# Moving the last two of a block's eight weight subtractions from GpSimd to VectorE

## The chip, the cores and the metric

The kernel runs on one core of one Trainium2 chip. The metric is device time in microseconds (us), from one execution to the next of the whole program. Five engines work side by side, each through its own queue of instructions, strictly in order: TensorE (PE for matmuls, PEld for weight loads in the profile), VectorE (DVE), ScalarE (ACT), GpSimd (POOL) and SyncE (SP, which here issues most DMAs). Semaphores order the work between them.

## The reference, cut to what matters

An attention layer whose queries are pooled in pairs is followed by a mixture of 8 experts. Each of the 2304 tokens goes to the one expert with the highest gate.

```python
x = softmax(scale * pool(q) @ k.T) @ v            # 4 x 8 heads -> 2304 tokens of 512
expert_idx = argmax(normalised(x) @ normalised(emb).T / tau)
for e in range(8):
    mask = expert_idx == e
    h = np.maximum(x[mask] @ w1[e], 0.0)          # 512 -> 1024
    out[mask] = gate_w[mask, None] * (h @ w2[e])  # 1024 -> 512
```

## The kernel before, in words

The attention stage fills the first 500 us and is not touched. Then the tokens, sorted by expert, are worked in blocks of 128 rows; every block belongs to one expert. With these inputs 21 blocks run, called block 0 to block 20 here. The first five belong to the most frequent expert and share one set of weights.

To keep precision, a float32 weight is held as two 16-bit tensors: a high part in fp16 and a low part in bf16, the difference. The weights of a block come from HBM as eight pieces of 128x1024 float32 (512 KB each): four of w1 and four of w2, in the staging tile `ld` (`st1`, `st2`). For each piece, `cast` (lines 775 to 784) makes the high part on ScalarE (line 782) and then the low part by a TENSOR_TENSOR subtraction (line 784), on GpSimd if the table `PCAST` names the piece and on VectorE otherwise. `PCAST` has six rows: w1 and w2 of the steady blocks (here from block 6 on), of blocks 0 and 1, and of block 5. Weights are converted anew for each block from block 5 on, also where the expert has not changed; the load of a piece (line 761) is skipped by a condition in that case. The last conversion is that of a block 21 which isn't run.

A block takes 96 matmuls of 128 columns, `mm1` (line 804, three products for the high and low parts), a `relu` in two halves, and 24 matmuls of 512 columns, `mm2` (line 827). Each half of the relu is one ScalarE instruction (line 810) and one VectorE instruction (line 811) that makes the low part of the hidden values; the second half's ScalarE instruction waits for the first half's VectorE instruction. `fin` scales the result on ScalarE (line 834) and scatters it by an indirect DMA from GpSimd's queue (line 835); `gather` (line 765) fetches the rows of a later block the same way.

The order is written out by hand in `seg`. In the round of block j it is: mm1 of block j+1; conversion of piece 0 of w1 of block j+2; fin of j-1; gather; piece 1; relu half 0 of j+1; pieces 2 and 3; loads of w1 of j+3; relu half 1 of j+1; mm2 of j; the four pieces of w2 of block j+1; loads of w2 of j+2. So TensorE does mm1 of j+1, mm2 of j, mm1 of j+2, mm2 of j+1, and so on. The converted weights have two sets of buffers (`ws`). After the last round each engine reads the number of blocks from memory (line 908) and branches (line 898): with 21 blocks the branch leads to mm2 and fin of block 20 alone.

Of the kernel before, what the change touches and what calls it, by code (L numbers as in the profile page):

```python
# [42 lines left out]
def attn_moe(ctx: ExitStack, tc: tile.TileContext, qt, kt, vt, emb, tau, w1, w2, out):  # L43
# [262 lines left out]
    RD = 3  # L306
    CUTS = [21, 22, 23, 24]
    WP = 4
    PCAST = [[2], [2], [0, 2, 3], [0, 1, 2, 3], [0, 1, 2, 3], [1]]
    VPOS = [0, 2, 3, 6]  # L310
    QPOS = [1, 2, 3, 3, 5, 7, 8]
    MPOS = [0, 0, 0, 7]
# [430 lines left out]
    def moe():  # L743
# [30 lines left out]
        def cast(j, which, *parts):  # L774
            if j >= NBLK or EB <= j < NS:
                return
            for i in parts:
# [4 lines left out]
                nc.scalar.activation(out=dh, in_=src, func=AF.Copy)  # L782
                eng = nc.gpsimd if i in PCAST[which + (2 if j < EB else 4 if j <= NS else 0)] else nc.vector
                eng.tensor_tensor(out=dl.bitcast(BF16), in0=src, in1=dh, op=ALU.subtract)  # L784
# [341 lines left out]
```

## Time and profile before

| what | value |
|---|---|
| median of 3 runs | 751.28 us (750.44 to 754.35) |
| profiled execution, its own time | 752.46 us |
| its span, first to last instruction | 750.7 us |
| mean granted TensorE clock, share of full speed | 0.955 |

The profile is of one execution. A row of the timeline gives a start (us from the span's start), a duration, the engine, the line of the kernel, the operation, what is written and read, and how many instructions of that kind in a row are merged; brackets give idle time before it and what ended it. Instructions of one engine can overlap by about a tenth of a us, so the cost of one in a row of its kind is read from starts, not from a single duration.

### The profile page before, as it was taken

Reading aid. Unit: us, or ns where it says so; the run is one execution under the profiler, and the core shown is the slowest. Engines: PE = TensorE matmul, PEld = TensorE weight load, DVE = VectorE, ACT = ScalarE, POOL = GpSimd, SP = SyncE. Lnnn points to the kernel's source line nnn. Section 1 sums busy time; section 2 is a strip of 40 time slices with the busy share of each in tenths; the row PEclk is TensorE's granted clock in tenths of the full one; section 3 lists DMA queues with packets and bytes.
Section 4 is the critical chain, followed back from the end, with each engine's and each line's share of the span. In section 5 each row is a group of like instructions: output and inputs, shape, how many; then the busy total and the mean of one; then the engine's idle time right before and its main releaser. Section 6 shows DMA issues by size and latency. Waiting matters only on the chain. (4 is left out here: it accounts for less than half of the span.)

```text
span 750.7 us, 21971 instructions
## 1 busy us (share of the span) xinstructions
PE 658.3 (88%) x8915; PEld 479.6 (64%) x8915; DVE 618.4 (82%) x975; ACT 480.3 (64%) x801; POOL 508.1 (68%) x347
## 2 busy tenths in 40 slices
PE   8798889998889988889989887869998998989883
PEld 3266767776667766677767666837756666665651
DVE  5579998889889888898887997471459999999986
ACT  2455667686676677577667465422647797777874
POOL 5567788887679877678857545652835766668654
PEclk9589999999999999999989998889999999999997
DMA  7724425557532569443375049519899655233581
GB/s 210 202 65 119 135 61 146 163 93 191 163 95 83 159 127 215 134 136 85 120 186 147 15 164 166 97 31 257 274 280 269 180 162 174 55 75 84 158 185 38
DMA packets 80524, 106.97 MB, mean 142 GB/s; under 512 B 50862, under 2 KB 54606, under 8 KB 80416
## 3 DMA queue, kind: packets, MB, share of 16 engines
q1 hardware_dynamic: 76160, 94.47, 48.1%
q0 software_dynamic: 3600, 11.03, 4.8%
q8 instruction: 72, 1.18, 0.7%
q14 instruction: 36, 0.29, 0.1%
q10 hardware_dynamic: 656, 0.00, 0.0%
HBM read 116.44 MB, written 10.23 MB: 169 GB/s over the span
## 5 line engine op out<-in xcount | busy, mean ns | idle before, releaser
L295 POOL TENSOR_TENSOR ar<-ar 128x576 f16<-128x576 f32 x175 | 232.6, 1340 | 112.4 <-ACT ar L293 112.1
L293 ACT ACTIVATE ar<-st 128x576 f32<-128x576 f32 x288 | 186.3, 650 | 120.3 <-PE st L291 112.8
L291 PE MATMUL st<-ar 128*128 128x288 f16 (+1 forms) x1152 | 195.6, 296 | 5.1 <-ACT ar L293 5.1
L784 DVE TENSOR_TENSOR ar<-ld,ar 128x1024 bf16<-128x1024 f32 x100 | 176.2, 1806 | 15.0 <-ACT ar L782 14.9
L370 PE MATMUL acc<-ar 128*128 128x65 f16 (+1 forms) x1440 | 167.3, 194 | 4.7 <-POOL ar L295 2.5
L368 PE MATMUL acc<-ar 128*128 128x65 f16 (+1 forms) x1440 | 167.4, 196 | 0.0
L369 PE MATMUL acc<-ar 128*128 128x64 f16 (+1 forms) x1440 | 167.0, 197 | 0.0
L259 DVE TENSOR_REDUCE mc<-m 128x1 f32<-128x512 f32 (+2 forms) x224 | 140.7, 653 | 26.3 <-PE m L248 17.7
L368 PEld LDWEIGHTS <-ar 128*128 128x128 bf16 (+1 forms) x1440 | 137.8, 99 | 34.8 <-issue 24.0
L782 ACT ACTIVATE ar<-ld 128x1024 f16<-128x1024 f32 x144 | 142.6, 1049 | 14.6 <-DMA ld<-in_w_dram 13.4
L369 PEld LDWEIGHTS <-ar 128*128 128x128 bf16 (+1 forms) x1440 | 137.7, 99 | 20.1 <-issue 2.1
L784 POOL TENSOR_TENSOR ar<-ld,ar 128x1024 bf16<-128x1024 f32 x44 | 99.5, 2268 | 66.6 <-ACT ar L782 53.5
L370 PEld LDWEIGHTS <-ar 128*128 128x128 f16 (+1 forms) x1440 | 138.0, 101 | 6.3 <-DVE ar L295 3.3
L804 PE MATMUL hps<-ar 128*128 128x128 f16 x2016 | 122.7, 220 | 17.6 <-POOL ar L784 9.5
L804 PEld LDWEIGHTS <-ar 128*128 128x128 f16 (+1 forms) x2016 | 115.3, 98 | 27.4 <-DVE ar L784 11.1
L291 PEld LDWEIGHTS <-ar 128*128 128x128 f16 (+1 forms) x1152 | 99.9, 100 | 37.4 <-issue 15.1
L827 PE MATMUL ops<-ar 128*128 128x512 f16 (+1 forms) x504 | 116.3, 388 | 7.4 <-DVE ar L784 3.9
L295 DVE TENSOR_TENSOR ar<-ar 128x576 f16<-128x576 f32 x113 | 113.6, 1006 | 0.5 <-ACT ar L293 0.5
L827 PEld LDWEIGHTS <-ar 128*128 128x128 f16 x504 | 49.3, 100 | 65.4 <-issue 9.6
L248 PE MATMUL m<-ar 128*128 128x512 f16 (+1 forms) x280 | 71.9, 319 | 10.3 <-DVE mc L259 8.8
L257 DVE CUSTOM_DVE_ANT_0 my<-m,my 128x512 bf16<-128x512 f32 x56 | 38.5, 688 | 24.8 <-PE m L248 13.8
L810 ACT ACTIVATE ar<-hps 128x512 f16<-128x512 f32 x38 | 22.6, 595 | 51.1 <-DVE ar L811 36.3
(180 smaller groups left out, 705.6 us busy)
## 6 DMA issues: line engine op xcount, KB each, us to landing
ld<-in_w_dram SPq DMA_DIRECT2D x156, 512.0 KB
ld<-in_q_dram SPq DMA_DIRECT2D x16, 576.0 KB
ld<-in_v_dram SPq DMA_DIRECT2D x16, 576.0 KB
ar<-ld SPq DMA_DIRECT2D x31, 288.0 KB
ld<-in_k_dram SPq DMA_DIRECT2D x15, 576.0 KB
ar<-ld SPq DMA_DIRECT2D x33, 144.0 KB
ar<-qhl SPq DMA_DIRECT2D x32, 144.0 KB
xs<-xh SPq DMA_DIRECT2D x13, 256.0 KB
```

Source lines behind the costliest of these rows:

```text
L248: nc.tensor.matmul(out=o, lhsT=qr[:, c:c + 128], rhs=kr[r], start=True, stop=True)
L259: nc.vector.tensor_reduce(out=mc[p, h][:, j, ts[0]:ts[0] + n], in_=m[:, 0:n * w].rearrange("p (t k) -> p t k", t=n), axis=AX.X, op=ALU.max)
L291: nc.tensor.matmul(out=st[:, a, 0:HQ], lhsT=KK[s][0:n, h, k, c * 128:(c + 1) * 128], rhs=QQ[s][0:n, h, k, a * HQ:(a + 1) * HQ], start=(k = ...
L293: nc.scalar.activation(out=e.rearrange("p (a q) -> p a q", a=2), in_=st[:, :, 0:HQ], func=AF.Exp, scale=1.0 / 16)
L295: return lambda: eng.tensor_tensor(out=EL[g % 2][:, c], in0=e, in1=hi(e), op=ALU.subtract)
L368: nc.tensor.matmul(out=a[r], lhsT=hi(e[:, w]), rhs=VV[s][:, c, h, 0:65], start=(x == 0), stop=False)
L369: nc.tensor.matmul(out=a[r, 0:64], lhsT=hi(e[:, w]), rhs=VV[s][:, c, h, 65:129], start=False, stop=False)
L370: nc.tensor.matmul(out=a[r], lhsT=el[:, w], rhs=VV[s][:, c, h, 0:65], start=False, stop=(x == NC - 1))
L782: nc.scalar.activation(out=dh, in_=src, func=AF.Copy)
L784: eng.tensor_tensor(out=dl.bitcast(BF16), in0=src, in1=dh, op=ALU.subtract)
L804: nc.tensor.matmul(out=hp[j, f][:, t * 128:t * 128 + 128], lhsT=wv(w, i % 2, c)[:, u], rhs=xt[:, 2 * c + i // 2], start=(c == 0 and t == 0 ...
L827: nc.tensor.matmul(out=op[j], lhsT=ht[:, c // 4, i // 2, (c % 4) * 128:(c % 4) * 128 + 128], rhs=wv(w, i % 2, c), start=(k == 0), stop=(k ...
```

## The change

Two entries of the table that says which pieces GpSimd subtracts are emptied: those of w1 and w2 of the steady blocks, which had one piece each (piece 2).

```diff
-    PCAST = [[2], [2], [0, 2, 3], [0, 1, 2, 3], [0, 1, 2, 3], [1]]
+    PCAST = [[], [], [0, 2, 3], [0, 1, 2, 3], [0, 1, 2, 3], [1]]
```

VectorE's program in the steady rounds, before (ar is the tile of the converted weights and hidden values, hps the result of mm1; L784 are subtractions, L811 the relu halves):

```order
L811 SCALAR_TENSOR_TENSOR ar<-hps,ar 128x512
L784 TENSOR_TENSOR ar<-ld,ar 128x1024
L811 SCALAR_TENSOR_TENSOR ar<-hps,ar 128x512
L784 TENSOR_TENSOR ar<-ld,ar 128x1024 x5
L811 SCALAR_TENSOR_TENSOR ar<-hps,ar 128x512
```

and after:

```order
L811 SCALAR_TENSOR_TENSOR ar<-hps,ar 128x512
L784 TENSOR_TENSOR ar<-ld,ar 128x1024 x2
L811 SCALAR_TENSOR_TENSOR ar<-hps,ar 128x512
L784 TENSOR_TENSOR ar<-ld,ar 128x1024 x6
L811 SCALAR_TENSOR_TENSOR ar<-hps,ar 128x512
```

Between the halves of a relu there are now two subtractions (pieces 2 and 3 of w1) where there was one (piece 3), and behind the second half six (four of w2, then pieces 0 and 1 of the next w1) where there were five.

GpSimd's program in the same rounds, before (out_dram is the result, xs the sorted rows in HBM):

```order
L784 TENSOR_TENSOR ar<-ld,ar 128x1024 x2
L835 DMA out_dram<-ar,six 2304x512
L765 DMA ar<-xs,gix 128x513
L784 TENSOR_TENSOR ar<-ld,ar 128x1024 x2
L835 DMA out_dram<-ar,six 2304x512
```

and after:

```order
L835 DMA out_dram<-ar,six 2304x512
L765 DMA ar<-xs,gix 128x513
L835 DMA out_dram<-ar,six 2304x512
L765 DMA ar<-xs,gix 128x513
L835 DMA out_dram<-ar,six 2304x512
```

Only the indirect DMAs of fin and gather stay there. TensorE's and ScalarE's programs are the same in both kernels.

## Rows read from the trace of the kernel before

**Rows 1.** The page: busy time of each engine, share of the span, instructions.

```profile
PE 658.3 (88%) x8915; PEld 479.6 (64%) x8915; DVE 618.4 (82%) x975; ACT 480.3 (64%) x801; POOL 508.1 (68%) x347
```

**Rows 2.** Windows (start:end, length): busy us per engine, granted clock, DMA share, GB/s.

```profile
533.20:554.30 21.10, 21.10 (x245) 15.44 (x243) 14.51 (x10) 12.31 (x15) 13.62 (x7) 1.00 0.91 231
554.30:593.50 39.20, 33.26 (x364) 23.20 (x362) 32.42 (x23) 30.26 (x36) 22.77 (x13) 1.00 0.90 268
593.50:723.70 130.20, 119.71 (x1322) 84.86 (x1320) 127.40 (x89) 98.81 (x117) 84.75 (x43) 1.00 0.46 129
```

**Rows 3.** Groups by line, 592.5 to 711.3: busy, mean ns | idle before.

```profile
L784 DVE TENSOR_TENSOR ar<-ld,ar 128x1024 bf16<-128x1024 f32 x61 | 108.8, 1827 | 2.2 <-ACT ar L782 2.2
...
L784 POOL TENSOR_TENSOR ar<-ld,ar 128x1024 bf16<-128x1024 f32 x20 | 45.0, 2248 | 32.1 <-ACT ar L782 31.8
```

**Rows 4.** Timeline of TensorE, 530 to 573.

```profile
533.21 5.34 PE L827 MATMUL ops<-ar 128*128 128x512 f16 x24
...
543.75 5.34 PE L827 MATMUL ops<-ar 128*128 128x512 f16 x24
...
564.53 0.84 PE L804 MATMUL hps<-ar 128*128 128x128 f16 x12 [2.15 <-POOL ar L784]
...
568.93 4.38 PE L827 MATMUL ops<-ar 128*128 128x512 f16 x19
```

**Rows 5.** Timeline of TensorE, 609 to 636.

```profile
612.56 0.84 PE L804 MATMUL hps<-ar 128*128 128x128 f16 x12 [1.17 <-POOL ar L784]
...
623.40 1.51 PE L804 MATMUL hps<-ar 128*128 128x128 f16 x24 [0.37 <-DVE ar L784]
```

**Rows 6.** Timeline of VectorE, 610 to 655.

```profile
610.02 3.57 DVE L784 TENSOR_TENSOR ar<-ld,ar 128x1024 bf16<-128x1024 f32 x1
...
623.86 1.21 DVE L784 TENSOR_TENSOR ar<-ld,ar 128x1024 bf16<-128x1024 f32 x1
625.00 0.68 DVE L811 SCALAR_TENSOR_TENSOR ar<-hps,ar 128x512 f16<-128x512 f32 x1
625.60 2.35 DVE L784 TENSOR_TENSOR ar<-ld,ar 128x1024 bf16<-128x1024 f32 x2
```

**Rows 7.** Timeline of VectorE in three short stretches, 614 to 631.

```profile
614.12 3.88 DVE L784 TENSOR_TENSOR ar<-ld,ar 128x1024 bf16<-128x1024 f32 x2
...
619.06 4.28 DVE L784 TENSOR_TENSOR ar<-ld,ar 128x1024 bf16<-128x1024 f32 x2
...
628.38 2.64 DVE L784 TENSOR_TENSOR ar<-ld,ar 128x1024 bf16<-128x1024 f32 x1 [0.44 <-ACT ar L782]
```

**Rows 8.** Timeline of GpSimd, 610 to 655.

```profile
610.37 2.14 POOL L784 TENSOR_TENSOR ar<-ld,ar 128x1024 bf16<-128x1024 f32 x1
613.64 2.14 POOL L784 TENSOR_TENSOR ar<-ld,ar 128x1024 bf16<-128x1024 f32 x1 [1.14 <-ACT ar L782]
```

**Rows 9.** Timeline of ScalarE, 544 to 562.

```profile
558.60 0.67 ACT L834 ACTIVATE ar<-ops,ar 128x512 f32<-128x512 f32 x1
559.17 1.05 ACT L782 ACTIVATE ar<-ld 128x1024 f16<-128x1024 f32 x1
560.12 0.58 ACT L810 ACTIVATE ar<-hps 128x512 f16<-128x512 f32 x1
560.60 2.00 ACT L782 ACTIVATE ar<-ld 128x1024 f16<-128x1024 f32 x2
```

**Rows 10.** The end: timeline of TensorE and GpSimd, 700 to 751.

```profile
723.61 5.34 PE L827 MATMUL ops<-ar 128*128 128x512 f16 x24
732.36 0.38 PE L827 MATMUL ops<-ar 128*128 128x512 f16 x1 [3.41 <-ACT ar L782]
736.68 7.10 PE L827 MATMUL ops<-ar 128*128 128x512 bf16 x23 [3.95 <-DVE ar L784]
...
744.91 1.01 POOL L835 DMA_INDIRECT out_dram<-ar,six  x1 [1.76 <-POOLq L898]
```

**Rows 11.** Instructions of line 898: queue, count, ns min/median/max, first and last start.

```profile
L898 PEldq COMPARE_BRANCH  x1: 4559/4559/4559, 727.7 to 727.7; - x1
```

## The prediction

> **What bounds the kernel now.** I read the page's busy times first, then windows over the expert stage, then the groups by line there, and last the timelines of single engines over two blocks.
>
> The page [rows 1] shows TensorE busy for 88% of the span and VectorE for 82%. That is a mean over stages, so windows come next [rows 2]. There are three different stretches. From 533.2 to 554.3 TensorE is busy all the time: 21.10 of 21.10 us. From 593.5 to 723.7 VectorE is busy for 127.40 of 130.20 us, 98%, and TensorE for 92%. Between them, from 554.3 to 593.5, the DMA engines are at 0.90 and move 268 GB/s, the weights of several experts one after another. The clock is 1.00 in all three.
>
> In the long last stretch VectorE is the bound. TensorE waits there inside mm1 for low parts that are not yet subtracted, 1.17 us for GpSimd's piece in one block and 0.37 us for VectorE's in the next [rows 5]. The second relu half on ScalarE waits for VectorE too.
>
> Is VectorE full of its own work? No. A subtraction alone takes 1.21 us; two in a row take 2.35, so each further one costs 1.14; a relu half is followed by the next instruction 0.60 us after its start [rows 6]. Yet the mean over 61 subtractions is 1.827 us [rows 3]. The long ones are those during which GpSimd subtracts. The one at 610.02 takes 3.57 us; GpSimd's runs from 610.37 to 612.51, and VectorE's ends 1.08 us later [rows 6, 8]. The others of the same two blocks show the same: the pair at 614.12 takes 3.88 where 2.35 is normal, the pair at 619.06 takes 4.28, the single one at 628.38 takes 2.64 [rows 7]. While GpSimd subtracts, VectorE's subtraction stands still. The lost time is 2.36 + 1.53 + 1.93 + 1.43 = 7.25 us in two blocks, 3.6 us a block. GpSimd's two subtractions take 2 x 2.25 us [rows 3], so most of what it works VectorE pays for.
>
> **The change, part by part.** It removes two subtractions a block from GpSimd and adds two to VectorE. What VectorE has to do in a block was 6 x 1.14 + 2 x 0.60 = 8.0 us of its own and 3.6 us of standing still, 11.6 us, and with its short waits the period of 11.9 us: mm2 of block 6 starts at 568.93 and mm2 of block 19 at 723.61 [rows 4, 10], 154.68 us for 13 blocks, 11.90 each. After the change it is 8 x 1.14 + 2 x 0.60 = 10.3 us, with no stop.
>
> Next is TensorE. Where it isn't held up, mm2 starts follow each other after 543.75 - 533.21 = 10.54 us [rows 4]. That is more than 10.3, so TensorE becomes the bound by a little. ScalarE has eight conversions at 0.95 us, two relu halves at 0.48 and a fin at 0.57, all by starts [rows 9]: 9.1 us. GpSimd keeps only its two indirect DMAs.
>
> Does the order let TensorE run through? Count from the end of mm1 of block j+1. ScalarE's relu half ends at about 0.8, VectorE's at 1.4, pieces 2 and 3 of the next w1 are subtracted by 3.7 (4.1 with the wait of 0.44 for ScalarE that [rows 7] shows). TensorE does mm2 of j meanwhile, 5.2 us, then starts the next mm1, which wants piece 2 after a quarter of its first half and piece 3 later; it would have to wait only if VectorE were over 3 us late. The second relu half and the four pieces of w2 are done at 4.3 and at about 9; the mm2 that needs them starts at 10.5. So nothing is left to wait for in the steady state, and VectorE, with 10.3 against 10.54, makes up a delay of 0.24 us in each block.
>
> The blocks: 13 x (11.90 - 10.54) = 17.7 us. At the entry mm1 of block 7 waits 2.15 us for GpSimd's piece, which itself waits for the load [rows 4]; VectorE would deliver it some 1.1 us earlier. Against that, with earlier work the loads between 560 and 590 come closer to being late; with the DMA at 0.90 I set 1.1 us against the 1.1 us and put the entry at nothing. Its ends are +2 and -4 us: all of the wait gained, or the whole gain of blocks 7 to 9 given back to the DMA (3 x 1.36).
>
> The end: before, mm2 of block 20 starts 8.75 us after mm2 of block 19 (732.36 against 723.61), because TensorE's branch takes 4.56 us from 727.7 on [rows 10, 11]. This stays. Then it stands for 4 us until VectorE has subtracted piece 0 of w2, which had two of GpSimd's pieces in front of it; the other 23 matmuls begin at 736.68 and take 7.10 us, in part at the low clock, 1.2 GHz. Now that piece is ready 5.4 to 5.8 us after the start of mm2 of block 19 (4.3 for the relu, and one subtraction), before the branch is through, and the others at 1.14 us intervals. So the 24 matmuls take 5.34 us from +8.75 and end at +14.1, where they ended at 743.78, +20.2. That is 6.1 us if the clock holds through the 3.4 us of the branch and 4.1 if it falls as before (7.10 against 5.34 x 23/24). The nearest row is the window from 554.3: TensorE is idle for 5.9 us of it in pieces and the clock stays at 1.00 [rows 2]; I take 6.1. ScalarE's four conversions of the unused block end by about +10.6 (the last staging piece is free at +9.2, and one conversion) and don't delay fin; the four extra subtractions there on VectorE hold up nobody. What follows the last matmul is the same.
>
> **The sum.** 17.7 + 6.1 = 23.8 us from the profiled execution's 752.46 is 728.7. The median is 1.18 us below that execution; the same gain from it would give 727.5. I predict 728.5 us.
>
> **A rule that speaks against a part of it.** The row: VectorE's instruction at 610.02 starts 0.35 us before GpSimd's at 610.37 and is still the one that is stretched, by 2.36 us [rows 6, 8]. The Trainium skill, "SBUF — State Buffer", section "Who interferes with whom", has both engines contend for one port pair when VectorE reads two inputs from SBUF, which agrees, but says that the one that issues first holds it and the other blocks. By that rule this one stretch would have another cause and would stay; by the rows it goes like the other three. It is the third rival below.
>
> **Rivals.**
> First, hand-offs between the engines keep the period above TensorE's own. For it: every block has the chain ScalarE, VectorE, ScalarE, VectorE in the relu, and today TensorE still waits 0.37 us where only VectorE delivers. Against it: those waits come from a VectorE that is late all the time. If about 0.6 us remain in each block, the period is 11.1, the gain 13 x 0.8 = 10.4, with 4.1 at the end 14.5 us: 738.0.
> Second, the loads bind in blocks 7 to 9: 4 us less, 724 to 733, or 732.7 from the sum. It lies inside the range.
> Third, the stretch of the instruction that started first isn't GpSimd's doing. Then 2.36 us in two blocks stay, VectorE needs 10.3 + 1.2 = 11.5 us a block, and 13 x 0.4 + 4.1 = 9.3 us are gained: 743.
> Fourth, and slower: the long subtractions come from VectorE's own traffic (the staging tile being filled while it is read, say) and not from GpSimd, so VectorE takes two more of the mean kind. Two at even 1.14 us added to a full engine are 2.28 us a block, 13 x 2.28 = 29.6 us: 782. It decides once eight subtractions average more than (11.9 - 1.2) / 8 = 1.34 us. Against it: each of the four long ones in two blocks lies on one of GpSimd's, and those that lie on none take 1.21.
> That the change doesn't move what it says is excluded by the order of the two programs.
>
> **How the numbers follow.** Forecast 0.70, first rival 0.15, second 0.07, third 0.04, fourth 0.04. About 0.5% (3.8 us) is what a measurement of this kernel can tell from no change. Faster by more takes in the forecast and the first three but for 0.03, which I leave for cases between the first rival and none: 0.93. Within 0.5%: 0.03. Slower: 0.04. The likeliest case alone reaches from 724 (entry +2, and the median's 1.18 with its rounding) to 735 (entry -4, clock falls). The range of 8 in 10 adds the first rival: 724 to 740.
>
> **What would show it.** In the changed profile: no L784 on GpSimd after 550; VectorE's subtractions all near 1.2 us there; mm2 starts 10.5 us apart with no idle time before L804; VectorE busy below TensorE; mm2 of block 20 in one piece right behind the branch. It would be wrong if mm2 starts were over 11 us apart, or if subtractions of over 2 us remained where GpSimd does none.

## The result and the profile after

The changed kernel takes 729.64 us (median of 4 runs, 727.7 to 735.48). The kernel before took 752.82 us beside it (median of 4); the ratio is 0.9718, 95% interval 0.9679 to 0.9758. The forecast was 728.5 us. The profiled execution took 728.07 us, with a span of 726.4 us against 750.7.

The windows of the kernel after (start:end, length, busy us of PE, PEld, DVE, ACT and POOL, granted clock, DMA share, GB/s), the third from the start of mm2 of block 6 to that of block 19:

```profile
554.30:593.50 39.20, 35.92 (x370) 25.36 (x372) 33.50 (x33) 33.08 (x39) 18.54 (x7) 0.96 0.94 275
593.50:705.00 111.50, 110.97 (x1275) 82.10 (x1284) 110.75 (x108) 99.82 (x118) 60.71 (x23) 1.00 0.57 150
...
569.20:706.22 137.02, 136.33 (x1551) 100.20 (x1561) 136.26 (x134) 122.48 (x145) 78.01 (x27) 1.00 0.62 167
```

In the long stretch TensorE was busy for 92% of the time [rows 2]; it is now busy for 110.97 of 111.50 us. VectorE is as full as before, but with two subtractions more a block.

TensorE's timeline of the kernel after:

```profile
569.20 5.34 PE L827 MATMUL ops<-ar 128*128 128x512 f16 x23
574.38 5.52 PE L804 MATMUL hps<-ar 128*128 128x128 f16 x96
579.74 5.34 PE L827 MATMUL ops<-ar 128*128 128x512 f16 x23
584.92 5.52 PE L804 MATMUL hps<-ar 128*128 128x128 f16 x96
590.28 5.34 PE L827 MATMUL ops<-ar 128*128 128x512 f16 x23
...
706.22 5.34 PE L827 MATMUL ops<-ar 128*128 128x512 f16 x23
712.44 5.34 PE L827 MATMUL ops<-ar 128*128 128x512 f16 x24 [0.88 <-ACT ar L782]
```

mm1 is one row of 96 matmuls now, with no wait inside it [rows 5 had them]; mm2 starts are 10.54 us apart, 13 times. mm2 of block 20 is in one piece.

VectorE's timeline of one block, and the groups by line from 592.5 to 698 (busy, mean ns | idle before):

```profile
628.53 6.89 DVE L784 TENSOR_TENSOR ar<-ld,ar 128x1024 bf16<-128x1024 f32 x6
635.34 0.68 DVE L811 SCALAR_TENSOR_TENSOR ar<-hps,ar 128x512 f16<-128x512 f32 x1
635.94 2.35 DVE L784 TENSOR_TENSOR ar<-ld,ar 128x1024 bf16<-128x1024 f32 x2
638.21 0.68 DVE L811 SCALAR_TENSOR_TENSOR ar<-hps,ar 128x512 f16<-128x512 f32 x1
```

```profile
L784 DVE TENSOR_TENSOR ar<-ld,ar 128x1024 bf16<-128x1024 f32 x82 | 95.1, 1214 | 0.8 <-ACT ar L782 0.6
...
L835 POOL DMA_INDIRECT out_dram<-ar,six x11 | 39.5, 3590 | 46.9 <-ACT ar L834 46.9
```

Six subtractions in a row take 6.89 us, 1.21 + 5 x 1.136. The mean of all is 1.214 us where it was 1.827 [rows 3]. So the same engine does a third more subtractions in less time: none is stretched any more. GpSimd's scatter (line 835) takes 3.59 us a piece. It is taken up under what was not expected.

### The profile page after: what moved, and what is told of

The parts are those of the page before. It is cut to its first block, busy times and chain, and to the rows that moved or that the text cites. A ratio compares the mean times of both kernels' runs of the same rounds, so it can differ in the third digit from the quotient of the medians.

```text
span 726.4 us, 21962 instructions
## 1 busy us (share of the span) xinstructions
PE 650.9 (90%) x8895; PEld 479.8 (66%) x8915; DVE 597.9 (82%) x1007; ACT 480.9 (66%) x801; POOL 469.0 (65%) x315
## 5 line engine op out<-in xcount | busy, mean ns | idle before, releaser
L784 DVE TENSOR_TENSOR ar<-ld,ar 128x1024 bf16<-128x1024 f32 x132 | 156.6, 1243 | 11.4 <-ACT ar L782 11.2
L782 ACT ACTIVATE ar<-ld 128x1024 f16<-128x1024 f32 x144 | 143.1, 1050 | 17.7 <-DMA ld<-in_w_dram 16.4
L804 PE MATMUL hps<-ar 128*128 128x128 f16 x2016 | 119.7, 222 | 4.3 <-DVE ar L784 2.3
L835 POOL DMA_INDIRECT out_dram<-ar,six x21 | 60.1, 2863 | 89.8 <-ACT ar L834 75.0
L827 PE MATMUL ops<-ar 128*128 128x512 f16 (+1 forms) x484 | 113.3, 384 | 1.9 <-ACT ar L782 0.9
L765 POOL DMA_INDIRECT ar<-xs,gix x24 | 42.5, 1769 | 14.5 <-issue 6.4
```

The costliest lines, as they stand in the source:

```text
L804: nc.tensor.matmul(out=hp[j, f][:, t * 128:t * 128 + 128], lhsT=wv(w, i % 2, c)[:, u], rhs=xt[:, 2 * c + i // 2], start=(c == 0 and t == 0 ...
L827: nc.tensor.matmul(out=op[j], lhsT=ht[:, c // 4, i // 2, (c % 4) * 128:(c % 4) * 128 + 128], rhs=wv(w, i % 2, c), start=(k == 0), stop=(k ...
```

## The experiments

**Half the change, the w1 piece.** Piece 2 of w1 goes to VectorE; w2's stays on GpSimd.

```diff
-    PCAST = [[], [], [0, 2, 3], [0, 1, 2, 3], [0, 1, 2, 3], [1]]
+    PCAST = [[], [2], [0, 2, 3], [0, 1, 2, 3], [0, 1, 2, 3], [1]]
```

> Half the change: piece 2 of w1 is subtracted on VectorE, piece 2 of w2 stays on GpSimd. If VectorE stands still while GpSimd subtracts, one stop a block is left, the shorter ones of before (1.53 and 1.43 us): VectorE needs 9 x ... that is 7 x 1.14 + 2 x 0.60 + 1.5 = 10.7 us a block against TensorE's 10.54, so mm2 starts 10.7 us apart, and with a stop in front of the last mm2 some 4 us above the full change: 731 to 735 us. If the long subtractions were VectorE's own doing, a move of one piece would not shorten them: about 11.9 us a block or more, 750 us.

Measured: 740.81 us (ratio 0.9884, interval 0.9821 to 0.9948), mm2 starts 11.24 us apart on average over blocks 6 to 19. That is 6 us above the range expected. The moved piece does shorten VectorE's mean, to 1.46 us, as it should if GpSimd causes the stops, but the price of the piece left behind is not the stop that it caused before. The timelines of one block show why (GpSimd, VectorE, TensorE):

```profile
631.04 6.98 POOL L784 TENSOR_TENSOR ar<-ld,ar 128x1024 bf16<-128x1024 f32 x1 [3.31 <-ACT ar L782]
...
630.29 5.75 DVE L784 TENSOR_TENSOR ar<-ld,ar 128x1024 bf16<-128x1024 f32 x5
635.97 0.67 DVE L811 SCALAR_TENSOR_TENSOR ar<-hps,ar 128x512 f16<-128x512 f32 x1
636.57 3.68 DVE L784 TENSOR_TENSOR ar<-ld,ar 128x1024 bf16<-128x1024 f32 x2
...
638.08 2.53 PE L827 MATMUL ops<-ar 128*128 128x512 bf16 x11 [1.99 <-POOL ar L784]
```

Here it is GpSimd that stands still. It begins while VectorE is in a row of five subtractions, which go on at their usual pace (5.75 us). GpSimd ends 2.05 us after the relu half behind the row has begun, which reads one of its inputs from PSUM, the memory that matmuls write; the piece took 2.14 before [rows 8]. So GpSimd seems to start its work only then, and the next VectorE subtraction stands still in turn. mm2 then waits 1.99 us for the late piece. Of the nine pieces from 592.5 to 698 three take 6.98 to 6.99 us like this one and one 4.71. The other five take 2.14 to 2.42, and in the three of them from 609.00 to 641.28 it is VectorE's row of five that is stretched instead, to 7.69, 7.70 and 8.30 us. Not two engines sharing, then, but one waiting for the other, either way round.

**The other half, the w2 piece.**

```diff
-    PCAST = [[], [], [0, 2, 3], [0, 1, 2, 3], [0, 1, 2, 3], [1]]
+    PCAST = [[2], [], [0, 2, 3], [0, 1, 2, 3], [0, 1, 2, 3], [1]]
```

> The other half: piece 2 of w2 on VectorE, piece 2 of w1 stays on GpSimd. The stops left are the longer ones (2.36 and 1.93 us): 7 x 1.14 + 2 x 0.60 + 2.15 = 11.3 us a block, 13 x 0.8 = 10 us above the full change, 738 to 742 us. By the rule that the engine that starts first is not held up, the stretch of 2.36 us, where VectorE started first, is not GpSimd's doing and would be seen in w1_moved as well, and the two halves would differ by less than 4 us.

Measured: 736.84 us (ratio 0.9852, 0.9791 to 0.9913), 1.2 us under the range; the mean distance of mm2 starts is 11.0 us. The two halves come out the other way round from what I had derived from the stops of before, but their intervals overlap, so which half is worth more isn't settled. Nor does their difference of 3.97 us decide on the rule that the engine that starts first is not held up: under 4 us was to speak for it. What speaks against it is that w1_moved has both subtractions between two relu halves in 2.34 us, at 616.32 and at 627.42, where the stretch of 2.36 us lay before. What else is shown: each gives about half of the 2.8%, and in both the piece left on GpSimd holds up TensorE from time to time, as in this row of TensorE's timeline:

```profile
630.70 4.14 PE L804 MATMUL hps<-ar 128*128 128x128 f16 x71 [2.35 <-POOL ar L784]
```

**GpSimd's reads put back, without the work.** Two subtractions a block on GpSimd on tensors that nobody else uses (AV holds an old one-hot matrix, XX old attention output).

```diff
                 eng.tensor_tensor(out=dl.bitcast(BF16), in0=src, in1=dh, op=ALU.subtract)
+                if j > NS and i == 2:
+                    nc.gpsimd.tensor_tensor(out=XX[:, 3].bitcast(BF16), in0=XX[:, 0:2].rearrange("p a b -> p (a b)"), in1=AV[:, 0:8].rearrange("p a b -> p (a b)"), op=ALU.subtract)
```

> The full change, plus two subtractions a block on GpSimd on tensors that nobody else uses (two inputs read from SBUF, the same size): no work is moved, nobody waits for them. If GpSimd's subtraction stops VectorE's, about 3.6 us a block come back: 10.3 + 3.6 = 13.9 us a block, 13 x 3.4 = 44 us above the full change, 765 to 780 us. If the long subtractions had another cause, nothing changes: 728 to 731 us.

Measured: 779.06 us in two runs (ratio 1.0397, 1.0319 to 1.0475). mm2 starts are 13.55 us apart on average (571.22 for block 6, 747.33 for block 19), 3.0 above the full change; 13.9 had been derived. Over 13 blocks that is 39 us of the 49; most of the rest lies at the end, where TensorE waits 6.3 us for VectorE before its last 23 matmuls. Groups by line from 592.5 to 698:

```profile
L784 DVE TENSOR_TENSOR ar<-ld,ar 128x1024 bf16<-128x1024 f32 x62 | 100.6, 1680 | 0.0
...
L806 PE MATMUL hps<-ar 128*128 128x128 f16 x685 | 46.7, 231 | 16.8 <-DVE ar L784 16.7
L786 POOL TENSOR_TENSOR xx<-xx,av 128x1024 bf16<-128x1024 f32 x17 | 45.0, 2649 | 0.9
```

Nobody waits for GpSimd's new instructions, and still VectorE's mean rises from 1.214 to 1.680 us, 3.7 us a block, and TensorE waits for VectorE. This is the experiment that shows the cause: the presence of GpSimd's subtraction is enough. VectorE's own subtractions are the same as in the full change.

**GpSimd busy, but only writing.**

```diff
                 eng.tensor_tensor(out=dl.bitcast(BF16), in0=src, in1=dh, op=ALU.subtract)
+                if j > NS and i == 2:
+                    nc.gpsimd.memset(XX[:, 5:9], 0.0)
```

> The full change, plus two GpSimd instructions a block that only write: a memset of 128x2048 float32 each, about as long as a subtraction. If VectorE is stopped by GpSimd's reads alone, VectorE's subtractions stay at 1.21 us and the time at 728 to 731 us; if any work of GpSimd in SBUF stops it, up to 3.6 us a block come back as in read2, 765 to 780 us.

Measured: 728.31 us (ratio 0.9702, 0.9641 to 0.9764), mm2 starts 10.54 us apart. Groups by line:

```profile
L784 DVE TENSOR_TENSOR ar<-ld,ar 128x1024 bf16<-128x1024 f32 x81 | 94.0, 1211 | 2.5 <-ACT ar L782 2.4
...
L786 POOL MEMSET xx<- 128x2048 f32 x20 | 36.4, 1820 | 0.6
```

GpSimd is busy for 3.6 us a block with the memsets, and VectorE's subtractions stay at 1.211 us. So it is not GpSimd's being busy in SBUF, the on-chip memory that holds these tiles; it is an operation of GpSimd's that reads there. Both of its inputs lay in SBUF; whether one would do was not run.

**One subtraction more on VectorE.**

```diff
                 eng.tensor_tensor(out=dl.bitcast(BF16), in0=src, in1=dh, op=ALU.subtract)
+                if j > NS and i == 2 and which == 0:
+                    nc.vector.tensor_tensor(out=XX[:, 3].bitcast(BF16), in0=XX[:, 0:2].rearrange("p a b -> p (a b)"), in1=AV[:, 0:8].rearrange("p a b -> p (a b)"), op=ALU.subtract)
```

> The full change, plus one subtraction of the same size a block on VectorE, on tensors that nobody else uses. If TensorE's own 10.54 us bounds a block now and VectorE has 0.24 us to spare, VectorE now needs 9 x 1.14 + 1.20 = 11.46 us and becomes the bound: 0.92 us a block, 13 x 0.92 = 12 us above the full change, 740 to 743 us. If hand-offs between the engines, and not either one's load, set the period, less than half of it shows: under 735 us.

Measured: 743.7 us (9 runs, ratio 0.9925, 0.9893 to 0.9956), 0.7 us above the range. TensorE's timeline:

```profile
642.92 3.47 PE L806 MATMUL hps<-ar 128*128 128x128 f16 x59 [0.70 <-DVE ar L784]
646.23 5.34 PE L829 MATMUL ops<-ar 128*128 128x512 f16 x24
...
657.64 5.34 PE L829 MATMUL ops<-ar 128*128 128x512 f16 x24
```

mm2 starts are 11.41 us apart; 11.46 had been worked out from 9 x 1.14 + 2 x 0.60. VectorE's load sets the period. Up to block 9 they are still 10.54 us apart. VectorE loses 0.87 us in a block, and mm2 of block 10 is only 0.78 us late (611.98), so VectorE was, by an estimate from these starts, 2.7 us ahead of need at block 6. From mm2 of block 6 to that of block 19 it is therefore 8.7 us more than with the full change, not 12; the profiled execution loses another 5.7 at the end, where the last 23 matmuls wait 2.65 us for VectorE and take 7.39.

**One subtraction fewer.** Piece 3 of w2 gets no new low part in the steady blocks; that part of the result is left out. TensorE's matmuls stay the same in number and shape.

```diff
+                if j > NS and i == 3 and which == 1:
+                    continue
                 eng.tensor_tensor(out=dl.bitcast(BF16), in0=src, in1=dh, op=ALU.subtract)
```

> The full change without the low part of piece 3 of w2 in the steady blocks: seven subtractions a block on VectorE, none on GpSimd (that part of the weights is left out). If TensorE is the bound, mm2 starts stay 10.54 us apart and the time stays within 2 us of the full change, 727 to 731 us; if VectorE still binds, up to 1.14 us a block are gained, 715 us.

Measured: 726.75 us (ratio 0.9701, 0.9654 to 0.9749), 0.3 us under the range; the full change has 0.9718. TensorE's timeline:

```profile
640.76 5.34 PE L829 MATMUL ops<-ar 128*128 128x512 f16 x24
...
651.30 5.34 PE L829 MATMUL ops<-ar 128*128 128x512 f16 x24
```

Still 10.54 us. TensorE is the bound after the change, and VectorE with eight subtractions just fits under it.

**All subtractions on VectorE.**

```diff
-    PCAST = [[], [], [0, 2, 3], [0, 1, 2, 3], [0, 1, 2, 3], [1]]
+    PCAST = [[], [], [], [], [], []]
```

> All subtractions of weights on VectorE, those of blocks 0, 1 and 5 too, where GpSimd has 3 and 4, and 4 and 1 pieces. Block 5 is converted while TensorE is busy without a gap (533 to 554 us), block 0 beside the last attention steps: no gain expected there from VectorE's stops. 726 to 732 us; the same as the full change. If GpSimd's stops cost time at the hand-over from attention too, 2 to 4 us less.

Measured: 728.17 us (ratio 0.9709, 0.9657 to 0.976). No difference from the full change, as expected.

**One subtraction fewer on GpSimd in attention.**

```diff
-    POOL_EL = [[1, 2, 4, 5, 6, 7], [0, 1, 3, 5, 8]]
+    POOL_EL = [[1, 2, 4, 6, 7], [0, 1, 3, 5, 8]]
```

> The full change, and in attention one of the six subtractions that GpSimd has in every even group (line 295, 128x576) goes to VectorE as well. There VectorE is at 86% of the time from 100 to 400 us and TensorE at 91%. One subtraction costs VectorE 0.75 us and saves it a stop of some 0.3 us on average (78 of them take 1.05 instead of 0.75 beside 122 of GpSimd's): 16 x 0.45 = 7 us more work in 450 us on an engine that isn't full, so 727 to 733 us. If the same rule as in the expert stage decides there, 3 to 6 us less.

Measured: 731.19 us (ratio 0.977, 0.9735 to 0.9805). No gain. Windows of this kernel and of the full change, 100 to 400 us (columns as above):

```profile
100.00:400.00 300.00, 269.66 (x4329) 209.63 (x4328) 264.28 (x503) 211.07 (x404) 216.42 (x155) 0.99 0.52 136
```

```profile
100.00:400.00 300.00, 271.79 (x4330) 210.80 (x4329) 259.28 (x493) 210.68 (x403) 231.18 (x166) 0.98 0.52 137
```

VectorE has 5.0 us more to do and GpSimd 14.8 less; VectorE isn't full there and TensorE is busy all the same. None of the versions run here beats the full change by more than the intervals.

## Why the prediction was right, step by step

- *VectorE stands still while GpSimd subtracts.* Shown by the two kernels that give GpSimd two instructions a block whose results nobody uses: subtractions, which read, stretch VectorE's again, memsets, which only write, don't. The fourth rival, VectorE's own traffic, falls with that, and with the mean of 1.214 us in the changed kernel.
- *Eight subtractions fit: 10.3 us.* Measured 6.89 us for six and 0.60 after a relu half, 10.28 from 628.53 to the next such row at 638.81; with nine the period is 11.41, with eight or seven it is TensorE's.
- *The blocks: 13 x 1.36 = 17.7 us.* From mm2 of block 6 to that of block 19 it was 154.68 us and is 137.02, 17.66. The first rival, hand-offs that keep 0.6 us a block, is not there.
- *The entry at nothing.* mm2 of block 6 starts at 569.20 where it was 568.93: 0.27 us later, in one execution each. The size came out, but by luck: one part was missing. The wait of 2.15 us for GpSimd's piece is gone, and ScalarE's first conversion for block 7, which waits for a load, starts 0.97 us later (558.61, before 557.64); these two the prediction had. It had TensorE's clock at 1.00 throughout, and the clock fell here: from 559.4 to 564.2 and on to 569.0 the granted clock was 0.87 and 0.78 (rows below), a mean between the two levels of 2.4 and 1.2 GHz, where before it was 1.00 in both. TensorE had stood for 0.78 and then 1.03 us from 558.9 to 561.0. The last 71 matmuls took 5.13 us; the 71 in the row of w2_moved above took 4.14. In all_dve and attn_less, which have the same subtractions in the steady blocks and kept 1.00 there, mm2 of block 6 starts 13.93 and 13.26 us after that of block 5, against 15.59 here and 14.64 before. By these rows the entry would have gained an estimated 0.7 to 1.4 us at the full clock. The second rival's loss of 4 us in blocks 7 to 9 didn't come, the starts are 10.54 us apart from block 6 on.
- *The end: 6.1 us.* It was 8.6: from mm2 of block 19 to the end of mm2 of block 20 it took 20.17 us and takes 11.56 (712.44 + 5.34 - 706.22). The step was mis-sized mainly in one number. I had the branch start 4.1 us into mm2; it starts 1.9 us into it (row below, 708.1) and takes 4.18 us. Why it comes earlier is open: in the other kernels here it starts 1.9 to 4.4 us into it as well. The clock held at 1.00, but not through the 3.4 us that were taken: TensorE stood for 0.88 us only. In all_dve, with the same subtractions in the last rounds, it stood for 2.08 and 1.41 us (rows below), the granted clock over the last 23 matmuls was 0.68 and they took 7.48 us; from mm2 of block 19 to the end it is 16.89 us there, not 11.56. The clock also fell in w2_moved, read2, write2 and one_more (0.72, 0.67, 0.75 and 0.69 over the last 23, which took 6.81 to 7.63 us) and for six matmuls in w1_moved. So the full clock at the end of the kernel after owes something to luck.
- *What follows the last matmul is the same.* It is not: from the end of mm2 of block 20 to the end of the span it was 6.9 us and is 8.6. GpSimd's last scatter takes 2.06 us instead of 1.01 [rows 10]. It runs beside VectorE's subtractions for the unused block, which end at 720.09, and ends 0.88 us after them. In w1_moved, the only other kernel where that is so, it takes 1.81 us and ends 0.89 us after them; in the others VectorE has finished and it takes 1.00 to 1.01. The remaining 0.65 us lie behind the scatter, and their cause is open.

Lines for the last three points. Kernel after, the entry, windows (columns as above) and TensorE's timeline:

```profile
559.40:564.20 4.80, 2.17 (x25) 1.60 (x25) 4.20 (x5) 4.80 (x8) 2.46 (x2) 0.87 1.11 319
564.20:569.00 4.80, 4.76 (x68) 4.77 (x69) 4.80 (x5) 4.80 (x6) 0.00 (x0) 0.78 0.97 341
```

```profile
564.24 5.13 PE L804 MATMUL hps<-ar 128*128 128x128 f16 x71 [0.63 <-DVE ar L784]
```

The end of all_dve, TensorE's timeline:

```profile
709.75 0.58 PE L827 MATMUL ops<-ar 128*128 128x512 f16 x1 [2.08 <-ACT ar L782]
711.74 7.48 PE L827 MATMUL ops<-ar 128*128 128x512 bf16 x23 [1.41 <-DVE ar L784]
```

Kernel after, the end (the branch: queue, count, ns min/median/max, start; then GpSimd's timeline):

```profile
L898 PEldq COMPARE_BRANCH  x1: 4179/4179/4179, 708.1 to 708.1; - x1
```

```profile
718.91 2.06 POOL L835 DMA_INDIRECT out_dram<-ar,six  x1 [3.60 <-ACT ar L834]
```

The sum by these pieces: -0.27 + 17.66 + 8.6 - 1.7 = 24.3 us, the difference of the two spans. The forecast was 23.8. Two misses of the end, +2.5 and -1.7, nearly cancel, so the closeness of the total is luck in that part; the 17.66 us of the blocks are not.

The third rival said that the stretch at 610.02, where VectorE had started 0.35 us before GpSimd, would stay. It went, so it was GpSimd's doing. The Trainium skill's rule that was weighed there ("SBUF — State Buffer", section "Who interferes with whom") is borne out in its kind, an exclusive hold by which one engine blocks, and by its limit to GpSimd's reads (write2). What the start times in the trace do not show is who will be the holder. VectorE lost at 610.02 after a relu half though it started first. In w1_moved GpSimd starts 0.75 us into VectorE's row at 630.29 and waits for four more subtractions of it, and 0.79 us into the row at 619.19 and is done in 2.42 us.

## What to carry to other kernels

When a fully busy engine has instructions of one kind with two very different durations, look up what the other engines did during the long ones before calling it full; taking the other engine's work over can cost less than letting it work alongside. The gain ends at the next engine's own period, which can be read from a stretch in the same trace where that engine runs without a gap. In attention, where VectorE was busy for 86% of the time, the one such move that was run gained nothing.

## What the runs showed that was not expected

GpSimd's indirect DMAs take longer beside long rows of subtractions on VectorE. The mean duration of the scatter from 592.5 to 698 is 1.58 us in the kernel before, with six subtractions a block and stops between them, and 3.59 with eight; with nine, 5.10 and for the gather 3.65:

```profile
L837 POOL DMA_INDIRECT out_dram<-ar,six x10 | 51.0, 5098 | 23.6 <-ACT ar L836 19.6 <-ACT ar L812 4.0
...
L765 POOL DMA_INDIRECT ar<-xs,gix x10 | 36.5, 3651 | 3.0 <-issue 3.0
```

With seven it is 1.45 us, although VectorE does one more than before:

```profile
L837 POOL DMA_INDIRECT out_dram<-ar,six x10 | 14.5, 1446 | 74.5 <-ACT ar L836 66.9 <-DMA ld<-in_w_dram 7.5
```

The count of subtractions is not the whole of it: in read2, with eight that are stretched, the scatter takes 1.24 us, and with seven VectorE's rows have gaps (5.9 us of waits for ScalarE in that window). The start and end of a long one say more. In the block of the kernel after that is shown above, VectorE's six subtractions start at 628.53 and the relu half behind them at 635.34. The scatter beside them is

```profile
632.33 3.98 POOL L835 DMA_INDIRECT out_dram<-ar,six  x1 [6.34 <-ACT ar L834]
```

and ends at 636.31, 0.97 us after that relu half has begun. Nine of the eleven scatters of this window take 3.57 to 4.37 us and end 0.96 to 0.98 us after the start of such a relu half; with nine subtractions all ten do (3.41 to 5.50 us). The other two, of 1.22 and 1.49 us, end within a row. So a long scatter looks like GpSimd's subtraction of 6.98 us in the first experiment: it is kept waiting until VectorE's row is broken. That it is the same hold is argued from this likeness; no run here varies what the scatter reads or writes.

Here the wait is hidden, since GpSimd has nothing else left to do; only the last scatter is on the path, and there it costs 1.05 us. What it would cost a kernel with more on GpSimd's queue was not run.
